# Issuing a kernel's loads from SyncE, ScalarE and GpSimd instead of from SyncE

## The chip, the core and the metric

One core of a Trainium2 chip runs the whole kernel. The time is the device time of one execution in microseconds (us). Each of the core's engines takes its instructions in order from a queue of its own: PE (TensorE), DVE (VectorE), ACT (ScalarE), POOL (GpSimd) and SP (SyncE, which only issues transfers here).

## The reference

Three layers follow each other. The first is gated linear attention over 4 batches, 8 heads, 768 tokens and a head dimension of 48:

```python
f = 1.0 / (1.0 + np.exp(-f_logit))
for t in range(S):
    state = f[:, :, t, :, None] * state + np.einsum('bhd,bhe->bhde', k[:, :, t], v[:, :, t])
    y[:, :, t] = np.einsum('bhd,bhde->bhe', q[:, :, t], state)
```

Its output, as a 3072 x 384 matrix x, goes through two MLP layers of width 2048:

```python
h = x @ w_in;  g = np.maximum(h, 0.0) + alpha * np.minimum(h, 0.0);  x = g @ w_out     # layer 0
h = x @ w_in;  g = h - np.tanh(h);                                   out = g @ w_out   # layer 1
```

The weights come as 64-bit floats; the activations and the output are 32-bit.

## The kernel before

The attention is cut into 24 steps. Step i handles 128 tokens (chunk c) of one batch b, with `c, b = divmod(i, 4)`, so steps 0 to 3 are the first chunk of the four batches. Their four outputs together are one tile of 512 tokens, on which layer 0 can start. MLP slots then run on PE (18 products of 128x512 each), and the later steps are spread among them.

A step has stages, and each engine does its part of them in order:

- `f` (`attn_f`): PE turns f (`ft`), ACT takes the exponential into the one buffer `gate` (L266) and adds 1 (L268), DVE scans it forward (`up`, L272) and backward (`down`, L280). The next step's L266 overwrites `gate`, so it waits for both scans.
- `k` (`attn_k`): PE turns k and q (`kt`, `qt`), DVE multiplies them into `kd` and `qd`.
- `s0`, `s1` (`attn_s`): PE forms the scores `sc` and turns `kd`. In steps 0 to 3 ACT copies the scores to `a` (L324) and POOL masks them (affine select, L325).
- `y0`, `y1` (`attn_y`): PE multiplies `a` with v; in steps 0 to 3 ACT and DVE write the result to x (L359, L360).
- `m` (`attn_m`): PE and DVE bring the state forward.

Weights come in 16 halves a layer (`load_w`, 768 KB each: the input half in four transfers for layer 0, the output half in one). `convert` turns such a half from 64-bit floats into two 32-bit parts: ACT takes the absolute value (`mag`, L54), DVE does five operations on it. Three raw buffers rotate, so the fourth half is loaded when the first has been converted.

A step's f, k, q and v are 192 KB each. In steps 0 to 3 f, k and q come as two transfers of 96 KB each, which a loop over `h` writes (heads `h::2`, four of the eight, with four tokens in a row, 768 bytes at a time):

```python
in_=a[b, h::2, t0:t0 + C, :].rearrange("p (t j) d -> p t (j d)", j=4)
```

From step 4 on each is one transfer of 192-byte rows (L175), into buffers that rotate over three steps: `f1`, `k1`, `q1` hold step 1, then step 4, then step 7. Steps 0 to 3 have their v loaded by `load_v` (one transfer of 144 KB in 192-byte rows and two of 24 KB in 64-byte rows).

Three things set the order. The table `PROLOGUE` says in which order the program's first parts are written: ("l", i) loads f, k and q of step i (from step 4 on v too), ("v", i) loads v, ("w", n) and ("c", n) load and convert half n of layer 0's weights, ("a", 0) loads alpha, and the rest are stages. A scheduler then places every engine's instructions by its own estimate of their times. And each transfer is given one of eight semaphores in turn; a transfer waits, in the queue of the engine that issues it, until the transfer that had its semaphore before has landed. SP and ACT share eight such semaphores (DMAHW0 to DMAHW7); POOL has eight of its own (DMASW0 to DMASW7).

Before the change SP issues every load and store but three: the second halves of step 0's f, k and q are issued by ACT.

Of the kernel before, what the change touches and what calls it, by code (L numbers as in the profile page):

```python
# [18 lines left out]
B, H, S, D = 4, 8, 768, 48  # L19
NT, DM, DFF = B * S, H * D, 2048  # L20
C = 128
# [11 lines left out]
HALF = 8  # L33

PROLOGUE = (
    ("l", 0), ("a", 0), ("l", 1), ("v", 0), ("l", 2), ("w", 0), ("v", 1), ("l", 3), ("v", 2), ("w", 1), ("w", 2),
    ("f", 0), ("k", 0), ("s0", 0), ("f", 1), ("s1", 0), ("y0", 0), ("y1", 0), ("m", 0), ("v", 3), ("k", 1), ("s0", 1),
    ("f", 2), ("s1", 1), ("y0", 1), ("y1", 1), ("m", 1), ("l", 4), ("k", 2), ("s0", 2), ("c", 0), ("f", 3), ("s1", 2),
    ("l", 5), ("y0", 2), ("y1", 2), ("m", 2), ("k", 3), ("s0", 3), ("l", 6), ("w", 3), ("s1", 3), ("y0", 3),
    ("y1", 3), ("c", 1), ("m", 3), ("f", 4),  # L40
)
GF = 256
# [28 lines left out]
def tile_main(tc, q, k, v, f_logit, w1_in, w1_out, alpha, w2_in, w2_out, out, flag):  # L71
    nc = tc.nc
    with ExitStack() as ctx:
# [23 lines left out]
            out=causal, in_=causal, compare_op=ALU.is_ge, fill=0.0,  # L97
# [13 lines left out]
        for b in range(2):  # L111
            t = const.tile([128, NP, 2, HW], F32, name=f"blocks{b}")
# [8 lines left out]
        alpha_raw = const.tile([FC, 128], F32, name="alpha_raw")  # L121


        def set_idle(t, nm):
            for a, b in ((4 * D, PAD), (PAD + 4 * D, H * HW)):
                nc.vector.memset(t[:, a:b], 30.0 if nm == "f" else 0.0)

        padded = {}
        for nm in ("f", "k", "q"):
            padded[nm] = []  # L130
            for j in range(NV):
                t = const.tile([128, H * HW], F32, name=f"{nm}{j}")
# [15 lines left out]
        def load_step(i):  # L148
            c, b = divmod(i, B)
            t0 = c * C  # L150
            s = {}
            for nm, a in (("f", f_logit), ("k", k), ("q", q), ("v", v)):
                if nm == "v" and c == 0:
                    continue
                if nm == "v":
                    t = s[nm] = ld.tile([128, H, D], F32, tag=nm, name=nm, bufs=NV)
                else:
                    if i == NV:
                        t = tp.tile([128, H * HW], F32, **{"f": dict(tag="g"), "k": dict(tag="g"), "q": dict(tag="neg", bufs=1)}[nm], name=nm)
                        set_idle(t, nm)  # L160
                    else:
                        t = padded[nm][i % NV]
                    if i < EARLY:

                        s[nm] = t[:, 0:2 * PAD].rearrange("p (h x) -> p h x", h=2)
                        for h in range(2):
                            (nc.scalar if i == 0 and h else nc.sync).dma_start(  # L167
                                out=s[nm][:, h, 0:4 * D],
                                in_=a[b, h::2, t0:t0 + C, :].rearrange("p (t j) d -> p t (j d)", j=4),
                            )  # L170
                        continue

                    s[nm] = t.rearrange("p (h x) -> p h x", h=H)
                    t = s[nm][:, :, 0:D]
                nc.sync.dma_start(out=t, in_=a[b, :, t0:t0 + C, :].rearrange("h t d -> t h d"))  # L175
            steps[i] = s

        def load_v(i):

            b = i  # L180
            s = steps[i]
            s["v"], s["v3"] = first_v[b % NV]
            nc.sync.dma_start(out=s["v"][:, :, 0:D], in_=v[b, 0:6, 0:C, :].rearrange("h t d -> t h d"))
            for h in range(2):
                nc.sync.dma_start(
                    out=s["v3"][:, h, :, D:64], in_=v[b, 6 + h, 0:C, :].rearrange("t (r d) -> t r d", r=3)
                )

# [2 lines left out]
        def load_w(m, g, half):  # L191
            wi, wo = ((w1_in, w1_out), (w2_in, w2_out))[m]
            f0 = g * GF
            a = stg.tile([128, 768, 2], I32, tag="raw", name="raw")
            raws[m, g, half] = a
            if half:
                nc.sync.dma_start(
                    out=a.rearrange("p (m e) w -> p m (e w)", m=2),
                    in_=wo[f0:f0 + GF].rearrange("(m p) e w -> p m (e w)", p=128),
                )  # L200
            elif m == 0:

                for h in range(2):
                    r0 = 64 * h
                    nc.sync.dma_start(
                        out=a[r0:r0 + D].rearrange("p (m f) w -> p m (f w)", m=3),
                        in_=wi[0:288, f0:f0 + GF].rearrange("(m p) f w -> p m (f w)", p=96)[D * h:D * h + D],
                    )
                    nc.sync.dma_start(
                        out=a[r0 + D:r0 + 64].rearrange("p (m f) w -> p m (f w)", m=3),  # L210
                        in_=wi[288 + D * h:288 + D * h + D, f0:f0 + GF].rearrange("(m p) f w -> p m (f w)", p=16),
                    )
            else:
                nc.sync.dma_start(
                    out=a.rearrange("p (m f) w -> p m (f w)", m=3),
                    in_=wi[:, f0:f0 + GF].rearrange("(m p) f w -> p m (f w)", p=128),
                )
# [340 lines left out]
        def stage(st, i, palloc=narrow):  # L558
            if st == "f":
                attn_f(i, palloc)  # L560
            elif st == "k":
                attn_k(i, palloc)
            elif st in ("s0", "s1"):
                attn_s(i, int(st[1]), palloc)
            elif st in ("y0", "y1"):
                attn_y(i, int(st[1]), palloc)
            else:
                attn_m(i, palloc)
# [4 lines left out]
        def convert(m, n):  # L573
            convert_a(m, *halves[n])
            convert_b(m, *halves[n])

        def load(m, n):
            load_w(m, *halves[n])

        for ev in PROLOGUE:  # L580
            if ev[0] == "c":
                convert(0, ev[1])
            elif ev[0] == "w":
                load(0, ev[1])
            elif ev[0] == "l":
                load_step(ev[1])
            elif ev[0] == "v":
                load_v(ev[1])
            elif ev[0] == "a":
                nc.sync.dma_start(out=alpha_raw, in_=alpha.rearrange("(c p) -> c p", p=128))  # L590
            else:
                stage(*ev, wide)

# [9 lines left out]
        for i in range(B, NC * B):  # L603
            c, b = divmod(i, B)

            if c < 3:
                t0, order = (0.7, 24.7)[c - 1] + 1.85 * b, tight_order
            else:
                t0, order = (c - 1) * FC + 3 * b + (2.5 if c == 3 else 0.5), wide_order
            for st, t in order:  # L610
                if ("f", i) not in PROLOGUE or st != "f":
                    put(t0 + t, stage, st, i)
            if i >= B + NV:
                put(t0 - NV * (1.85 if c < 3 else 3) + 0.8, load_step, i)
        first = sum(ev[0] == "c" for ev in PROLOGUE)
        when = {2: 0, 3: 1.2, 4: 2.0, 5: 3.2, 6: 4.2, 7: 5.4}
        for n in range(2 * NG):
            t = when.get(n, 7.5 + 1.5 * (n - NG)) if n >= first else -0.3
# [10 lines left out]
        for n, (g, half) in enumerate(halves):  # L629
            t = max(last + 6 + 1.5 * n, last + 2 * g + 2 * half + 2.2)  # L630
# [132 lines left out]
def kernel(tc, *args):  # L763
    nc = tc.nc
    with tc.tile_pool(name="flag", bufs=1) as fp:
        flag = fp.tile([1, 1], I32, name="flag")
        tile_main(tc, *args, flag)
        strong = nc.values_load(flag, min_val=0, max_val=1)
        with tc.If(strong > 0):
            tile_general(tc, *args)  # L770
# [33 lines left out]
```

## Time and profile before

| | us |
|---|---|
| median of 3 runs | 978.15 |
| lowest and highest | 977.35, 979.97 |
| the profiled execution, its whole time | 977.85 |
| its span, first to last instruction | 975.8 |

The span is what the trace covers; 2.05 us of the profiled execution lie outside it. In the trace an engine's line such as L359 is a line of the kernel, "SPq" and "ACTq" are the queues of SP and ACT while they issue a transfer, and PEclk is the granted share of TensorE's clock.

### The profile page before, as it was taken

How to read it: one execution, taken by the hardware profiler on the slowest of the kernel's cores; microseconds unless marked ns; L12 is line 12 of the kernel's file. 1: busy time of each engine (PE TensorE's matmuls, PEld its weight loads, DVE VectorE, ACT ScalarE, POOL GpSimd, SP SyncE). 2: the span in 40 equal slices, each digit the busy share in tenths (PEclk: the TensorE clock that was granted, in tenths of full speed). 3: DMA queues.
4: the chain of work that ended last, by engine and by line, in shares of the span. 5: the costliest groups of instructions: out<-in, count | busy, mean ns of one | idle time of the engine just before them, and what ended most of it. 6: DMA issues, size and time to landing. Idle time of an engine off the chain costs nothing.

```text
span 975.8 us, 13398 instructions
## 1 busy us (share of the span) xinstructions
PE 943.2 (97%) x5299; PEld 779.7 (80%) x5299; DVE 560.9 (57%) x926; ACT 408.4 (42%) x721; POOL 9.6 (1%) x24
## 2 busy tenths in 40 slices
PE   5598999999999999999999999999999999999997
PEld 5577787888888887888888888888888888888896
DVE  5589998566655565456444899953343433433432
ACT  3265556444444443444344665532232332322222
POOL 2000000000000000000000000000000000000000
PEclk9789999999999999999999999999999999999999
DMA  4897845042421232112022336330030110200201
GB/s 103 149 190 162 148 107 116 9 110 44 82 50 33 49 85 47 25 36 62 8 67 65 122 105 194 98 65 0 1 66 1 22 44 0 33 1 1 33 1 35
DMA packets 154277, 62.68 MB, mean 64 GB/s; under 512 B 123856, under 2 KB 141664, under 8 KB 154208
## 3 DMA queue, kind: packets, MB, share of 16 engines
q1 hardware_dynamic: 153812, 61.47, 28.4%
q8 instruction: 43, 0.70, 0.3%
q10 hardware_dynamic: 396, 0.29, 0.1%
q14 instruction: 26, 0.21, 0.1%
HBM read 49.55 MB, written 10.22 MB: 61 GB/s over the span
## 4 chain that ended last, share of the span: by engine, by line
PE 90%; DMA 4%; DVE 3%; SPq 2%; issue 0%; ACT 0%; ACTq 0%; DVEq 0%
PE acc L511 40%; PE h L451 13%; PE h L452 13%; PE h L453 13%; PE sc L319 2%; PE y L366 2%; PE y L342 2%; DMA k<-in_k_dram 2%; PE kt L248 1%; DMA raw<-in_moe_w_in_dram 1%; PE m L401 1%; PE qt L248 1%; PE ft L248 1%; SPq L167 1%; PE kr L305 1%; DMA f<-in_f_logit_dram 1%
## 5 line engine op out<-in xcount | busy, mean ns | idle before, releaser
L451 PE MATMUL h<-x,wih 128*128 128x512 f32 x576 | 228.6, 397 | 2.4 <-DMA x<-x 2.4
L452 PE MATMUL h<-x,wih 128*128 128x512 f32 x576 | 225.0, 391 | 0.0
L453 PE MATMUL h<-x,wil 128*128 128x512 f32 x576 | 225.0, 391 | 0.0
L511 PE MATMUL acc<-gh,wol 128*128 128x512 f32 x528 | 206.8, 393 | 1.8 <-DVE wol L233 1.8
L511 PE MATMUL acc<-gl,woh 128*128 128x512 f32 x528 | 207.6, 393 | 0.0
L511 PE MATMUL acc<-gh,woh 128*128 128x512 f32 x528 | 201.4, 396 | 0.9 <-ACT woh L232 0.9
L472 ACT CAST gh<-g 128x512 fp32r<-128x512 f32 x192 | 119.2, 621 | 139.4 <-DVE g L464 73.6
L473 DVE TENSOR_TENSOR gl<-g,gh 128x512 fp32r<-128x512 f32 x192 | 132.1, 688 | 76.5 <-ACT gh L472 67.9
L464 DVE TENSOR_TENSOR g<-h,g 128x512 f32<-128x512 f32 x96 | 66.2, 689 | 146.0 <-ACT g L463 146.0
L459 DVE SCALAR_TENSOR_TENSOR g<-neg,alpha_neg,g 128x512 f32<-128x512 f32 x96 | 72.0, 750 | 123.1 <-ACT neg L458 123.0
L463 ACT ACTIVATE g<-h 128x512 f32<-128x512 f32 x96 | 57.5, 599 | 174.8 <-PE h L453 174.8
L451 PEld LDWEIGHTS h<-x,wih 128*128 128x128 f32 x576 | 108.2, 188 | 24.6 <-DMA x<-x 2.8
L453 PEld LDWEIGHTS h<-x,wil 128*128 128x128 f32 x576 | 108.1, 188 | 23.2 <-DVE dec L65 0.2
L452 PEld LDWEIGHTS h<-x,wih 128*128 128x128 f32 x576 | 108.3, 188 | 20.9
L511 PEld LDWEIGHTS acc<-gh,wol 128*128 128x128 f32 x528 | 99.3, 188 | 22.6 <-DVE wol L233 1.9
L511 PEld LDWEIGHTS acc<-gh,woh 128*128 128x128 f32 x528 | 99.1, 189 | 22.9 <-ACT woh L232 1.5
L511 PEld LDWEIGHTS acc<-gl,woh 128*128 128x128 f32 x528 | 99.6, 189 | 20.4 <-DVE gl L473 0.4
L457 ACT ACTIVATE g<-h 128x512 f32<-128x512 f32 x96 | 57.5, 598 | 130.5 <-PE h L453 129.6
L458 ACT ACTIVATE neg<-h 128x512 f32<-128x512 f32 x96 | 56.9, 593 | 0.0
L272 DVE TENSOR_TENSOR_SCAN up<-gate,reset 128x516 f32<-128x516 f32 x24 | 29.5, 1231 | 10.5 <-ACT gate L268 9.9
L319 PEld LDWEIGHTS sc<-qd,kd 48*128 48x128 f32 x384 | 26.5, 193 | 9.0 <-issue 4.6
L319 PE MATMUL sc<-qd,kd 48*128 48x128 f32 x384 | 31.4, 291 | 1.2 <-DVE qd L294 1.2
(99 smaller groups left out, 805.8 us busy)
## 6 DMA issues: line engine op xcount, KB each, us to landing
raw<-in_moe_w_out_dram SPq DMA_DIRECT2D x16, 768.0 KB
raw<-in_moe_w_in_dram SPq DMA_DIRECT2D x8, 768.0 KB
raw<-in_moe_w_in_dram SPq DMA_DIRECT2D x16, 288.0 KB
x1d<-o SPq DMA_DIRECT2D x24, 192.0 KB
x1raw<-x1d SPq DMA_DIRECT2D x6, 768.0 KB
f<-in_f_logit_dram SPq DMA_DIRECT2D x20, 192.0 KB
k<-in_k_dram SPq DMA_DIRECT2D x20, 192.0 KB
q<-in_q_dram SPq DMA_DIRECT2D x20, 192.0 KB
```

The lines of the kernel that those rows point to most:

```text
L319: nc.tensor.matmul(out=sc[h][:, p], lhsT=s["kd"][r, p], rhs=s["qd"][r, p], start=True, stop=True)
L451: nc.tensor.matmul(out=h, lhsT=a, rhs=xh[:, r], start=(r == 0), stop=False)
L452: nc.tensor.matmul(out=h, lhsT=a, rhs=xl[:, r], start=False, stop=False)
L453: nc.tensor.matmul(out=h, lhsT=b, rhs=xh[:, r], start=False, stop=(r == 2))
L457: nc.scalar.activation(out=g, in_=h, func=ACTF.Relu)
L458: nc.scalar.activation(out=neg, in_=h, func=ACTF.Relu, scale=-1.0)
L459: nc.vector.scalar_tensor_tensor(out=g, in0=neg, scalar=alpha_neg[:, fc:fc + 1], in1=g, op0=ALU.mult, op1=ALU.add)
L463: nc.scalar.activation(out=g, in_=h, func=ACTF.Tanh)
L464: nc.vector.tensor_tensor(out=g, in0=h, in1=g, op=ALU.subtract)
L472: nc.scalar.copy(out=gh, in_=g)
L473: nc.vector.tensor_tensor(out=gl, in0=g, in1=gh.bitcast(F32), op=ALU.subtract)
L511: nc.tensor.matmul(out=t, lhsT=a, rhs=b, start=first and i == 0, stop=final and i == 2)
```

## The change

The loads are shared out among three engines. SP keeps the other loads of f, k and q, v from step 4 on, and all stores. ACT issues the second halves of f, k and q of steps 0 and 1 and the first input half of layer 0's weights. POOL issues v of steps 0 to 3, alpha and the other weights of layer 0. The weights of layer 1 stay on SP (`eng` is `nc.sync` where `m` is 1). `PROLOGUE` lists the first loads in another order and converts the first half two places later.

```diff
 PROLOGUE = (
-    ("l", 0), ("a", 0), ("l", 1), ("v", 0), ("l", 2), ("w", 0), ("v", 1), ("l", 3), ("v", 2), ("w", 1), ("w", 2),
+    ("l", 0), ("l", 1), ("w", 0), ("v", 0), ("v", 1), ("l", 2), ("v", 2), ("l", 3), ("w", 1), ("a", 0), ("w", 2),
     ("f", 0), ("k", 0), ("s0", 0), ("f", 1), ("s1", 0), ("y0", 0), ("y1", 0), ("m", 0), ("v", 3), ("k", 1), ("s0", 1),
-    ("f", 2), ("s1", 1), ("y0", 1), ("y1", 1), ("m", 1), ("l", 4), ("k", 2), ("s0", 2), ("c", 0), ("f", 3), ("s1", 2),
-    ("l", 5), ("y0", 2), ("y1", 2), ("m", 2), ("k", 3), ("s0", 3), ("l", 6), ("w", 3), ("s1", 3), ("y0", 3),
+    ("f", 2), ("s1", 1), ("y0", 1), ("y1", 1), ("m", 1), ("l", 4), ("k", 2), ("s0", 2), ("f", 3), ("s1", 2),
+    ("l", 5), ("c", 0), ("y0", 2), ("y1", 2), ("m", 2), ("k", 3), ("s0", 3), ("l", 6), ("w", 3), ("s1", 3), ("y0", 3),
...
-                            (nc.scalar if i == 0 and h else nc.sync).dma_start(
+                            (nc.scalar if i < 2 and h else nc.sync).dma_start(
...
-            nc.sync.dma_start(out=s["v"][:, :, 0:D], in_=v[b, 0:6, 0:C, :].rearrange("h t d -> t h d"))
+            nc.gpsimd.dma_start(out=s["v"][:, :, 0:D], in_=v[b, 0:6, 0:C, :].rearrange("h t d -> t h d"))
             for h in range(2):
-                nc.sync.dma_start(
+                nc.gpsimd.dma_start(
...
+            eng = nc.sync if m else nc.scalar if (g, half) == (0, 0) else nc.gpsimd
             if half:
-                nc.sync.dma_start(
+                eng.dma_start(
...
-                nc.sync.dma_start(out=alpha_raw, in_=alpha.rearrange("(c p) -> c p", p=128))
+                nc.gpsimd.dma_start(out=alpha_raw, in_=alpha.rearrange("(c p) -> c p", p=128))
```

The other transfers of `load_w` change in the same way to `eng.dma_start`. One line is added, so lines from L197 on are one higher in the changed kernel.

Three queues change at the places below. In a row, DMA is a transfer, out<-in are the program's tiles with their numbers, and [waits ...] names the semaphores that the instruction waits for.

On ACT, at the start of the program, before: three transfers, then the table load and the exponential of step 0 (`gate<-ft`).

```order
L167 DMA f0_129<-in_f_logit_dram 128x1x192
L167 DMA k0_138<-in_k_dram 128x1x192
L167 DMA q0_147<-in_q_dram 128x1x192
L266 ACT_TABLE_LOAD
L266 ACTIVATE gate_109<-ft_224 128x4x128 [waits PE_49]
```

The same place after the change: seven more transfers stand ahead of the table load. Six of them wait for an earlier transfer, and the last one's semaphore was that of `q1_150`, the second half of step 1's q.

```order
L167 DMA f1_132<-in_f_logit_dram 128x1x192
L167 DMA k1_141<-in_k_dram 128x1x192 [waits DMAHW1_49]
L167 DMA q1_150<-in_q_dram 128x1x192 [waits DMAHW3_49]
L206 DMA raw_181<-in_moe_w_in_dram 48x3x512 [waits DMAHW5_49]
L210 DMA raw_181<-in_moe_w_in_dram 16x3x512 [waits DMAHW7_49]
L206 DMA raw_181<-in_moe_w_in_dram 48x3x512 [waits DMAHW1_49]
L210 DMA raw_181<-in_moe_w_in_dram 16x3x512 [waits DMAHW3_49]
L267 ACT_TABLE_LOAD
L267 ACTIVATE gate_109<-ft_224 128x4x128 [waits PE_49]
```

So the first exponential has moved behind the landing of step 1's q. Further down on ACT, the exponentials of steps 1 and 2 now both stand ahead of the first copy of scores; before, only that of step 1 did.

On SP, from step 4's f on, before (`f1`, `k1`, `q1` and `v_425` are step 4, `f2` and so on step 5, `f0` and so on step 6):

```order
L175 DMA f1_132<-in_f_logit_dram 128x8x48
L175 DMA k1_141<-in_k_dram 128x8x48
L175 DMA q1_150<-in_q_dram 128x8x48
L175 DMA v_425<-in_v_dram 128x8x48
L175 DMA f2_135<-in_f_logit_dram 128x8x48
```

And after:

```order
L175 DMA f1_132<-in_f_logit_dram 128x8x48
L175 DMA v_425<-in_v_dram 128x8x48
L175 DMA v_493<-in_v_dram 128x8x48
L175 DMA f0_129<-in_f_logit_dram 128x8x48
L175 DMA f2_135<-in_f_logit_dram 128x8x48
L175 DMA k0_138<-in_k_dram 128x8x48
L175 DMA q0_147<-in_q_dram 128x8x48
L175 DMA v_571<-in_v_dram 128x8x48
L175 DMA k1_141<-in_k_dram 128x8x48
L175 DMA q1_150<-in_q_dram 128x8x48
```

Seven whole transfers, v of steps 4, 5 and 6, f of steps 6 and 5 and k and q of step 6, have moved between step 4's f and step 4's k. On PE the first product of step 4's `kt` stands ahead of step 3's scores, in both orders.

On POOL, after the memsets of the start, before: the masks of step 0 and of step 1, each two instructions.

```order
L142 MEMSET vb2_165 128x6x48
L325 AFFINE_SELECT a_265<-a_265 128x512 [waits Activation_49] x2
L325 AFFINE_SELECT a_356<-a_356 128x512 [waits Activation_49] x2
```

And after, from the end of the first weights on: ahead of these rows stand nine transfers of v, alpha and the four of the second input half, so 15 with the row of `raw_222`.

```order
L198 DMA raw_222<-in_moe_w_out_dram 128x2x768 [waits DMASW6_49]
L326 AFFINE_SELECT a_265<-a_265 128x512 [waits Activation_49] x2
L183 DMA va0_156<-in_v_dram 128x6x48 [waits DMASW7_49,PE_49]
L185 DMA vb0_157<-in_v_dram 128x3x16 [waits DMASW0_49,PE_49]
L185 DMA vb0_157<-in_v_dram 128x3x16 [waits DMASW1_49,PE_49]
L326 AFFINE_SELECT a_356<-a_356 128x512 [waits Activation_49] x2
```

Step 0's mask has moved behind 15 transfers, and step 1's behind three more (v of step 3, into the buffer that step 0 leaves).

## Rows read from the trace of the kernel before

**Rows 1.** The page's head: span and PE's busy time.

```profile
span 975.8 us, 13398 instructions
PE 943.2 (97%) x5299; PEld 779.7 (80%) x5299; DVE 560.9 (57%) x926; ACT 408.4 (42%) x721; POOL 9.6 (1%) x24
```

**Rows 2.** Windows by stage: length; busy time of PE, PEld, DVE, ACT, POOL; clock, DMA share, GB/s.

```profile
0.00:60.00 60.00, 38.81 (x469) 33.61 (x470) 32.43 (x82) 20.05 (x36) 9.64 (x24) 0.86 0.73 136
60.00:120.00 60.00, 54.95 (x396) 43.91 (x396) 57.33 (x99) 35.35 (x64) 0.00 (x0) 0.97 0.87 163
120.00:700.00 580.00, 580.00 (x3208) 474.06 (x3207) 368.13 (x594) 268.62 (x481) 0.00 (x0) 1.00 0.27 67
```

**Rows 3.** The chain that ended last, 41 to 51 us: start, us, what.

```profile
41.23 8.33 DMA k<-in_k_dram
49.70 0.73 PE kt L248 x4
```

**Rows 4.** Timeline of PE around steps 1, 3 and 4 and the first MLP product.

```profile
12.25 0.98 PE L253 MATMUL ft<-ident,f 128*64 128x128 f32 x13 [0.47 <-DMA f<-in_f_logit_dram]
50.35 2.08 PE L319 MATMUL sc<-qd,kd 48*128 48x128 f32 x16
59.04 0.48 PE L451 MATMUL h<-x,wih 128*128 128x512 f32 x1
```

**Rows 5.** Windows inside the loads of the start, columns as in rows 2.

```profile
6.00:8.00 2.00, 2.00 (x18) 1.74 (x16) 0.00 (x0) 0.20 (x1) 0.00 (x0) 1.00 0.27 92
10.00:12.00 2.00, 1.30 (x18) 0.85 (x16) 1.97 (x5) 0.00 (x0) 0.00 (x0) 1.00 0.28 91
36.00:50.00 14.00, 9.87 (x159) 8.92 (x156) 9.62 (x17) 6.34 (x12) 1.23 (x2) 0.98 1.06 189
42.00:44.00 2.00, 2.00 (x46) 2.00 (x46) 0.62 (x3) 1.83 (x3) 1.20 (x2) 1.00 0.98 334
50.00:56.00 6.00, 5.62 (x50) 4.73 (x50) 5.07 (x9) 2.56 (x5) 1.23 (x2) 0.51 1.24 180
58.00:60.00 2.00, 2.00 (x22) 1.74 (x19) 1.75 (x4) 1.36 (x3) 0.00 (x0) 1.00 1.47 179
```

**Rows 6.** Timeline of SP's queue where it issues step 6's loads.

```profile
51.94 1.13 SPq L175 DMA_DIRECT2D f<-in_f_logit_dram  x1
53.12 1.11 SPq L175 DMA_DIRECT2D k<-in_k_dram  x1
```

**Rows 7.** Timeline of ACT, 0 to 60 us.

```profile
3.25 1.28 ACT L266 ACT_TABLE_LOAD   x1 [3.25 <-issue]
7.80 0.60 ACT L266 ACTIVATE gate<-ft 128x512 f32<-128x512 f32 x1 [3.26 <-PE ft L253]
8.43 0.72 ACT L268 ACTIVATE gate<-gate,ones 128x512 f32<-128x512 f32 x1
15.07 1.06 ACT L324 COPY a<-sc 128x512 f32<-128x512 f32 x2
...
21.60 0.48 ACT L359 CAST x<-y 128x384 fp32r<-128x384 f32 x1 [2.06 <-PE y L358]
...
36.90 0.48 ACT L359 CAST x<-y 128x384 fp32r<-128x384 f32 x1 [11.14 <-PE y L358]
...
45.78 0.48 ACT L359 CAST x<-y 128x384 fp32r<-128x384 f32 x1 [1.57 <-PE y L358]
...
57.48 0.48 ACT L359 CAST x<-y 128x384 fp32r<-128x384 f32 x1 [3.89 <-PE y L358]
```

**Rows 8.** Timeline of DVE: first and last of eight instructions of one step.

```profile
37.41 0.56 DVE L360 TENSOR_TENSOR x<-y,x 128x384 fp32r<-128x384 f32 x1 [8.84 <-ACT x L359]
...
42.12 0.14 DVE L285 COPY inv<-carry 128x4 f32<-128x4 f32 x1
```

**Rows 9.** Timeline of POOL: its last memset and its first masks.

```profile
3.52 0.34 POOL L142 MEMSET vb<- 128x288 f32 x1
15.71 2.74 POOL L325 TENSOR_SCALAR_AFFINE_SELECT a<-a 128x512 f32<-128x512 f32 x2 [11.85 <-ACT a L324]
23.61 1.23 POOL L325 TENSOR_SCALAR_AFFINE_SELECT a<-a 128x512 f32<-128x512 f32 x2 [5.16 <-ACT a L324]
```

**Rows 10.** Timeline of DVE beside POOL's first masks.

```profile
17.95 0.53 DVE L285 COPY inv<-carry 128x4 f32<-128x4 f32 x1
```

**Rows 11.** Line L183's issues from SP: duration in ns, least, median, most.

```profile
L183 SPq DMA_DIRECT2D va<-in_v_dram x4: 401/720/1873, 11.3 to 38.2; - x4
```

## What the change is expected to do

> **What bounds the kernel now.** I read the page's head first. PE is busy 943.2 of 975.8 us [rows 1], so the question is where its 32.6 idle microseconds lie. The windows by stage answer it [rows 2]: 60 − 38.81 = 21.2 us idle in the first 60 us, 60 − 54.95 = 5.05 us in the next 60, and none from 120 to 700, where PE is busy 580 of 580 us. No transfer is late there, so nothing that the change does to loads can help there. In 60 to 120 us DVE works 57.33 of 60 us: what comes late into that stretch finds no slack to make it good. The start alone is at stake, and its end is the moment at which step 3's x lets the first MLP product begin: the x copy at 57.48 [rows 7], `h` at 59.04 [rows 4]. From there the program is one dense run, so I let a shift of step 3's x pass whole into the end time.
>
> What does that x wait for? The chain that ended last [rows 3] shows PE waiting for step 4's k, not for a thing of step 3: the transfer, issued at 41.23, takes 8.33 us, and `kt` starts at 49.70. The reader should see in the timeline that the 16 score products `sc` of step 3 begin at 50.35 [rows 4], right behind `kt`: PE works in order, and the order puts step 4's `kt` ahead of step 3's scores. So step 3's x hangs on the landing of step 4's k, 57.48 − 49.70 = 7.8 us behind it.
>
> And what keeps that k? The windows inside the loads [rows 5]. While only first-step halves are loaded, 91 to 92 GB/s move at a DMA share of 0.27 to 0.28: about a quarter of the 16 DMA engines' time, since a transfer's slowest dimension is four heads. A half of 96 KB then takes 98.3 KB / 92 GB/s = 1.07 us, and 24 of them 25.7 us, whoever issues them. Weights run at 334 GB/s with a share of 0.98. The whole transfers of 192-byte rows run at 179 to 180 GB/s with shares above 1: there the DMA engines are full, and SP issues one about every 1.18 us [rows 6], which is their pace (196.6 KB / 179 GB/s = 1.10 us).
>
> **The change part by part.**
>
> *SP's order, the term that decides.* Seven whole transfers are moved ahead of step 4's k. Each takes 1.10 us at 179 GB/s, or 1.18 us by the pitch of SP's issues: 7 × 1.14 = 8.0 us. PE still has step 4's `kt` ahead of step 3's `sc`. So `kt` goes from 49.70 to 57.7, and step 3's x from 57.48 to 65.5.
>
> *What could pay some of it back.* SP no longer issues v and weights, so it can reach step 4's f sooner than now. But the DMA engines have to move the same bytes first. The busiest quarter of them carries 25.7 us of halves and its share of the rest: 3.54 MB (three weight halves of 786 KB, four v of 197 KB, f and k of step 4), 18.7 us at the 189 GB/s of the mixed stretch from 36 to 50 us [rows 5]. The 8th half landed at 12.25 [rows 4], 3.7 later than 8 × 1.07, which is start and latency. 25.7 + 18.7 + 3.7 = 48.1, against a landing at 49.6 now: 1.5 us are idle there to be won. With the weights at 334 and the rest at 179 GB/s it is 7.1 + 6.6 instead of 18.7, and 6.5 us to be won; the mixed rate is the nearer row. A second refund: from 50 to 56 us the granted clock is 0.51, the lower level of 1.2 GHz, after PE had waited for transfers [rows 5]. If PE comes out of its wait at the full level, the 7.1 us from `sc` to x might lose 3 us. A surcharge: if the fourth weight half, on POOL, gets ahead of k, 786 KB / 334 GB/s = 2.4 us more. The bounds of this part are 8.0 − 6.5 − 3.0 = −1.5 and 8.0 + 2.4 = +10.4 us. I take +8.0: before, too, PE came out of its waits at the lower level, and the 1.5 and the 2.4 work against each other.
>
> The Trainium skill has a rule on this ("DMA: Bandwidth & Descriptors", "Issuing engines are not separate DMA queues"): transfers from any engine end up on the same 16 DMA engines, and several issuers save only the issuing time. The trace agrees as far as SP's issues go at the pace of the bytes; taken alone the rule gives a change of nothing, the third rival below.
>
> *ACT: ten transfers ahead of the first exponential.* The last of them waits for the landing of step 1's second q, the 12th half. The 8th (step 1's second f) had landed at 12.25 [rows 4], four more take 4 × 1.07 = 4.3: 16.5 us. One issue of 0.40 [rows 11] and the table load of 1.28 [rows 7] give step 0's `gate` at 18.2, not 7.80: 10.4 us later. Then the exponentials of steps 1 and 2 stand ahead of the first copy of scores, and each waits for both scans of the step before, which is a run of eight DVE instructions, 37.41 to 42.26 or 4.8 us [rows 8]. So step 2's `gate` is at 18.2 + 9.7 = 27.9, the copies to `a` come 1.32 (0.60 + 0.72) later at 29.2, and x of step 0, which lies 21.60 − 15.07 = 6.5 us behind them now [rows 7], comes between 32.4 (copies 1.06, masks 1.23, about 1 for the products) and 35.7. The next three x follow at a pitch between the DVE's 5.2 (4.8 and some 0.4 for the state) and the 8.9 us from 36.90 to 45.78 [rows 7]; the middle is 7. Step 3's x by this chain alone: 34.0 + 21 = 55.0, bounds 48.0 and 62.4. All are below 65.5, so the delayed exponential costs nothing as long as k binds; without that cover it would cost up to 62.4 − 57.5 = +4.9.
>
> *POOL: 15 transfers ahead of step 0's mask.* They hold 5264 separate runs (v: 3 × 768 and 6 × 384; alpha 16; weights 384 and 256). Nothing in before shows what POOL takes to issue. From below: SP's issues of one such v transfer take 0.40 to 1.87, median 0.72 us [rows 11], at least 0.5 ns a run. From above: POOL's own work per element, 0.34 us for 288 elements (1.2 ns) and up to 2.74 us for a pair of masks of 512 (2.7 ns) [rows 9]. With POOL free at 3.9, and 0.5 us a transfer: 3.9 + 7.5 + 5264 × 0.5 to 2.7 ns = 14 to 26 us. Step 0's `a` is not there before 29, so the issues are hidden; I take nothing. They show from the point at which the mask comes later than 65.5 − 21 − 5.9 (mask to x, 15.71 to 21.60) = 38.6 us, which is 5.2 ns a run.
>
> *v, alpha and the first conversion.* v now comes past SP's queue, and the first half is converted two places later. Both lie inside the steps' pitch, whose bounds of 5.2 and 8.9 us hold them; the wait for k covers both.
>
> The sum is 977.85 (the profiled execution's own time, 0.3 below the median of 978.15) + 8.0 = 985.9, or **986**.
>
> **The rivals.**
>
> *POOL issues slowly.* For it: DVE and POOL do disturb each other. A COPY of 128×4 elements on DVE took 0.53 us beside POOL's mask [rows 10], and 0.14 elsewhere [rows 8]; DVE is busy most of the time in which POOL would issue. Against it: nothing in before prices such an issue. At 8 ns a run the mask starts at 3.9 + 7.5 + 42.1 = 53.5, x of step 0 at 59.4, of step 3 at 80.4: +22.9, or about 1001. It decides from 5.2 ns a run. The Trainium skill speaks for this one ("SBUF — State Buffer", the "DVE blocks DMA" trap under "SBUF: two separate sides"): the runs of a GpSimd transfer are written by its own cores, which DVE can lock out. No transfer of before is issued by POOL, so no row shows it.
>
> *Faster.* The DMA share in the first 16 us is far below 1 (0.27 and 0.28 where I looked [rows 5]). If three queues fill that idle share with weights and v better than my 1.5 us, step 4's k lands by 49.8 in spite of its seven forerunners, and PE comes to `sc` at the full clock. Then ACT's chain decides: step 3's x at 55.0 down to 48.0, −2.5 to −9.5, about 973. It decides only when all 8 us are hidden. Against it: the busy quarter has no such idle time.
>
> *No change.* The seven transfers are hidden so, but ACT's late chain eats the gain: x of step 3 within 2.9 us of 57.48, some 977 to 979.
>
> **How the numbers follow.** Forecast 0.54, slow POOL 0.21, faster 0.12, no change 0.13. About 0.3% (2.9 us) is what a measurement of this kernel can tell from no change. The likeliest case's own range is 976.4 to 988.3 (−1.5 and +10.4). The range for 8 in 10 reaches down to 976, which leaves out the faster case, and up to 1002, where the slow POOL case stands at 8 ns a run; what is dearer, some 0.08, is left out. Faster 0.12, same 0.13, slower 0.75, since the forecast and the slow POOL are both slower.
>
> **What would show it.** Right: PE waits at step 4's `kt` for a transfer of k until about 57; step 0's `gate` stands at 18 to 21; the first `h` comes at about 67; 120 to 700 us is as full as now. Wrong: step 4's k lands by 50; or PE's long wait is for POOL's `a`, with POOL's issues longer than 2 us each; or the gap at ACT's first exponential is long past 21, so that the last wait is for a scan rather than for k. If the first `h` shifts and the end doesn't shift with it, the step "no slack in 60 to 120" is the one that failed.

## The result, and the profile after

The changed kernel took 988.22 us (median of 4 runs, 987.13 to 988.82), beside 979.06 for the kernel before in the runs taken with it: a ratio of 1.0092, 95% interval 1.0068 to 1.0115. It is slower, 2.2 us above the forecast of 986 and inside its range. The profiled execution took 988.82 us with a span of 987.0, so 11.2 us of span lie between the two traces. By the medians it is 9.2 us: single executions of the kernel before lie between 975.75 and 981.67 us, so 2 us between two spans are within their spread.

The page's head of the changed kernel, as [rows 1]:

```profile
span 987.0 us, 13426 instructions
PE 945.2 (96%) x5299; PEld 780.4 (79%) x5299; DVE 561.9 (57%) x926; ACT 409.6 (41%) x721; POOL 41.9 (4%) x73
```

PE does the same 5299 products. Its idle time grew from 32.6 to 41.8 us. The windows by stage, as [rows 2]:

```profile
0.00:60.00 60.00, 35.36 (x422) 29.14 (x422) 30.45 (x76) 18.31 (x32) 23.49 (x43) 0.86 0.66 148
60.00:120.00 60.00, 56.83 (x434) 45.95 (x434) 55.61 (x100) 33.78 (x61) 10.57 (x18) 0.97 0.75 139
120.00:700.00 580.00, 573.67 (x3173) 468.99 (x3171) 369.50 (x594) 270.27 (x484) 7.85 (x13) 1.00 0.28 69
```

The first 60 us hold 3.5 us less of PE's work, and behind 120 us, where PE had been full, 6.33 us are idle now. Where the start went is read from the timelines. ACT first (ACTq is its queue while it issues a transfer):

```profile
11.20 0.37 ACTq L206 DMA_DIRECT2D raw<-in_moe_w_in_dram  x1
13.41 0.32 ACTq L210 DMA_DIRECT2D raw<-in_moe_w_in_dram  x1
16.98 0.32 ACTq L206 DMA_DIRECT2D raw<-in_moe_w_in_dram  x1
20.01 0.32 ACTq L210 DMA_DIRECT2D raw<-in_moe_w_in_dram  x1
20.36 1.28 ACT L267 ACT_TABLE_LOAD   x1 [20.36 <-DMA raw<-in_moe_w_in_dram]
21.66 0.60 ACT L267 ACTIVATE gate<-ft 128x512 f32<-128x512 f32 x1
...
36.61 0.48 ACT L360 CAST x<-y 128x384 fp32r<-128x384 f32 x1 [2.75 <-PE y L359]
...
48.15 0.48 ACT L360 CAST x<-y 128x384 fp32r<-128x384 f32 x1
...
55.45 0.46 ACT L360 CAST x<-y 128x384 fp32r<-128x384 f32 x1
...
63.74 0.48 ACT L360 CAST x<-y 128x384 fp32r<-128x384 f32 x1 [5.55 <-PE y L359]
```

Against [rows 7] the first exponential has gone from 7.80 to 21.66 us, and step 0's x from 21.60 to 36.61. Each of the last four issues takes only 0.3 us, but stands 2.2 to 3.6 us behind the one before it: ACT is held by the semaphore of an earlier transfer. Step 3's x has gone from 57.48 to 63.74, only 6.3 us. The timeline of PE, as [rows 4]:

```profile
38.49 0.40 PE L254 MATMUL ft<-ident,f 128*64 128x128 f32 x2 [0.90 <-DMA f<-in_f_logit_dram]
39.74 0.98 PE L254 MATMUL ft<-ident,f 128*64 128x128 f32 x13 [0.84 <-DMA f<-in_f_logit_dram]
...
55.66 0.27 PE L249 MATMUL kt<-ident,k 128*128 128x128 f32 x1
55.86 1.16 PE L320 MATMUL sc<-qd,kd 48*128 48x128 f32 x16
...
65.20 0.48 PE L452 MATMUL h<-x,wih 128*128 128x512 f32 x1
...
106.36 1.16 PE L320 MATMUL sc<-qd,kd 48*128 48x128 f32 x16 [0.72 <-DVE qd L295]
...
123.55 1.16 PE L320 MATMUL sc<-qd,kd 48*128 48x128 f32 x16 [2.49 <-DVE qd L295]
...
129.39 0.76 PE L452 MATMUL h<-x,wih 128*128 128x512 f32 x1 [3.84 <-DMA x<-x]
```

The line at 55.66 is the one on which the forecast rested: step 4's `kt` starts with no wait ahead of it. Its k was there by then. PE's waits at 38.49 and 39.74 are for step 3's f, which had landed at 32.6 in the kernel before. The chain that ended last says the same: three f transfers, and then work. ACT's early transfers and its late first exponential are not on it.

```profile
2.93 9.64 DMA f<-in_f_logit_dram
12.59 14.31 DMA f<-in_f_logit_dram
...
27.56 12.14 DMA f<-in_f_logit_dram
...
39.74 0.92 PE ft L254 x13
```

The first `h` moved by 65.20 − 59.04 = 6.16 us, the end by 11.2. Of the 5.0 us in between, 4.0 are seen as waits of PE behind `h`: the rows of such waits up to 145 us add up to 9.0 us after the change (the last three above and 0.89, 0.90 and 0.20) and to 5.0 before. Before the change there are four of them, the last two being these:

```profile
87.06 1.17 PE L511 MATMUL acc<-gh,wol 128*128 128x512 f32 x3 [1.81 <-DVE wol L233]
119.68 0.47 PE L451 MATMUL h<-x,wih 128*128 128x512 f32 x1 [2.36 <-DMA x<-x]
```

POOL's issues, last, whose price nothing had shown:

```profile
17.88 0.82 POOL L183 DMA_DIRECT2D va<-in_v_dram  x1 [5.05 <-issue]
...
20.18 0.53 POOL L591 DMA_DIRECT2D alpha_raw<-in_moe_alpha_dram  x1
...
27.34 0.74 POOL L198 DMA_DIRECT2D raw<-in_moe_w_out_dram  x1
32.85 2.14 POOL L326 TENSOR_SCALAR_AFFINE_SELECT a<-a 128x512 f32<-128x512 f32 x2 [4.78 <-ACT a L325]
```

A transfer of 768 runs takes POOL 0.82 us, one of 16 runs 0.53: 0.3 us for 752 runs, or 0.4 ns a run. POOL was done at 28.1, with gaps of 4.3, 5.1 and 4.4 us between its issues, and then waited for ACT's `a`.

### The profile page after: what moved, and what is told of

Read it like the earlier page. It is cut to its first block, busy times and chain, and to the rows that moved or that the text cites. A ratio compares the mean times of both kernels' runs of the same rounds, so it can differ in the third digit from the quotient of the medians.

```text
span 987.0 us, 13426 instructions
## 1 busy us (share of the span) xinstructions
PE 945.2 (96%) x5299; PEld 780.4 (79%) x5299; DVE 561.9 (57%) x926; ACT 409.6 (41%) x721; POOL 41.9 (4%) x73
## 4 chain that ended last, share of the span: by engine, by line
PE 88%; DMA 5%; DVE 5%; ACT 1%; issue 1%; SPq 1%; DVEq 0%; ACTq 0%
PE acc L512 39%; PE h L452 13%; PE h L454 13%; PE h L453 13%; DMA f<-in_f_logit_dram 4%; PE sc L320 2%; PE y L367 2%; DMA x<-x 2%; PE y L343 1%; PE kt L249 1%; PE m L402 1%; PE qt L249 1%; PE ft L249 1%; DVE down L281 1%; PE kr L306 1%
```

## The experiments

Three theories went into the runs. **A**: ACT's late first exponential sets the start. **B**: a second queue (POOL's weights above all) takes the DMA engines from SP's f, k and q. **C**: the forecast's, step 4's k lands late behind seven transfers. All ratios are to the kernel before, on the same chip. "x0" and "x3" are the x casts of steps 0 and 3 on ACT, `h` the first MLP product; times are from each run's profile. The intervals are 0.1 to 0.35% wide to either side, so the ratios alone don't tell two parts of 0.2% apart.

| run | what it is | ratio, 95% interval | x0 | x3 | h | span |
|---|---|---|---|---|---|---|
| before | | 1 | 21.60 | 57.48 | 59.04 | 975.8 |
| after | | 1.0092, 1.0068 to 1.0115 | 36.61 | 63.74 | 65.20 | 987.0 |
| e1 | after, weights but the first on SP | 1.0065, 1.0039 to 1.0091 | 36.09 | 63.12 | 64.23 | 982.4 |
| e3 | after, ACT's part undone | 1.0097, 1.0066 to 1.0127 | 46.13 | 64.73 | 65.84 | 985.3 |
| e4 | after, table of before | 1.0054, 1.0037 to 1.0071 | 37.30 | 61.15 | 63.12 | 982.1 |
| e5 | before, table of after | 1.0040, 1.0024 to 1.0056 | 28.21 | 60.80 | 63.10 | 980.1 |
| f1 | before, v and alpha on POOL | 1.0017, 1.0003 to 1.0031 | 28.67 | 58.47 | 60.44 | 977.3 |
| f2 | before, weights but the first on POOL | 1.0027, 1.0014 to 1.0040 | 21.81 | 57.29 | 60.14 | 979.5 |
| f3 | before, ACT's part alone | 1.0015, 1.0003 to 1.0027 | 35.05 | 58.29 | 60.25 | 979.7 |
| f4 | before, first conversion later | 0.9972, 0.9953 to 0.9990 | 22.90 | 54.14 | 56.23 | 972.9 |
| f5 | before, first loads in the new order | 1.0013, 1.0001 to 1.0024 | 28.39 | 62.11 | 63.43 | 977.8 |
| g1 | after, first loads in the old order | 1.0114, 1.0081 to 1.0147 | 36.74 | 62.86 | 63.97 | 987.4 |
| g7 | after, step 4's k and q on ACT | 1.0166, 1.0139 to 1.0193 | 45.55 | 69.52 | 70.63 | 989.3 |
| g5 | e1, step 4's k and q on ACT | 1.0157, 1.0122 to 1.0192 | 47.04 | 71.17 | 72.28 | 990.1 |

### One part undone, or one half of the change alone (e1, e3, e4, e5)

**e1**, on the changed kernel:

```diff
-            eng = nc.sync if m else nc.scalar if (g, half) == (0, 0) else nc.gpsimd
+            eng = nc.scalar if (m, g, half) == (0, 0, 0) else nc.sync
```

> All weight halves but the first go back from GpSimd to SyncE, the rest stays as after the change. Theory A (ScalarE's late first exponential decides): the first exponential still stands at 20 to 22 us, the first MLP product at 64 to 66, about 986 to 989. Theory B (weights on a queue of their own take the DMA engines from f, k and q on SyncE's queue): step 3's f lands by 35 instead of 39.7, the x<-x transfers get short again, 979 to 982. Theory C (the prediction: step 4's k stands behind seven transfers): the seven are still there, 986 to 990.

It came out between: 984.47 us, with an interval that overlaps that of the changed kernel. Step 3's f was no longer waited for (`ft` at 37.01 without a wait), as B said. But then PE waited where C had put the wait, for step 4's k (timeline of PE):

```profile
56.30 0.30 PE L249 MATMUL kt<-ident,k 128*128 128x128 f32 x1 [3.79 <-DMA k<-in_k_dram]
```

So B's wait was real, and C's stands right behind it: taking one away laid the other bare, and step 3's x moved only from 63.74 to 63.12. Most of the 4.6 us between the two spans lies behind `h` (span less `h` is 918.2 instead of 921.8): the wait for x<-x at the second slot is 1.09 instead of 3.84 us.

**e3**, on the changed kernel:

```diff
-                            (nc.scalar if i < 2 and h else nc.sync).dma_start(
+                            (nc.scalar if i == 0 and h else nc.sync).dma_start(
...
-            eng = nc.sync if m else nc.scalar if (g, half) == (0, 0) else nc.gpsimd
+            eng = nc.sync if m or (g, half) == (0, 0) else nc.gpsimd
```

> Step 1's second halves and the first weight half go back from ScalarE to SyncE, v, alpha and the other weights stay on GpSimd. Theory A: the first exponential is back at about 8 us, the first MLP product at 58 to 60, 978 to 983. Theory B: step 3's f still lands near 39, 985 to 988. Theory C: k of step 4 stands ahead of most of the seven here, so 978 to 980.

987.77 us: nothing gained that could be measured, though the first exponential is back at 7.89 us (by f3, below, ACT's part is worth 0.15%, less than this interval can tell). A as the only cause has fallen, and so has C, which had asked for 978 to 980: step 4's k is issued right behind its f again, at 40.96 as against 41.23 before, and PE does not wait for it. B's forecast for this run fits. Timeline of PE and of SP's queue:

```profile
39.69 0.66 PE L254 MATMUL ft<-ident,f 128*64 128x128 f32 x2 [7.66 <-DMA f<-in_f_logit_dram]
```

```profile
21.56 5.85 SPq L167 DMA_DIRECT2D q<-in_q_dram  x2
27.45 6.27 SPq L167 DMA_DIRECT2D f<-in_f_logit_dram  x2
...
40.96 2.13 SPq L175 DMA_DIRECT2D k<-in_k_dram  x1
```

Two halves of 96 KB keep SP's queue for 5.85 and 6.27 us, just while POOL issues its weights (22.0 to 29.4 us in this run). With those weights on SP (e1) step 3's two f halves took this:

```profile
25.16 1.35 SPq L167 DMA_DIRECT2D f<-in_f_logit_dram  x2
```

The changed kernel differs from e1 in the weights' queue alone, and there they took this:

```profile
26.92 4.64 SPq L167 DMA_DIRECT2D f<-in_f_logit_dram  x2
```

PE, which works in order, has step 3's `ft` ahead of step 0's `y` here, so even step 0's x waited for that f (46.13). One more delay shows here. ACT's copies to `a` end at 17.8, but POOL masks step 0 only at 29.41, right behind its last issue; in the changed kernel ACT's lateness covers that.

```profile
28.66 0.74 POOL L198 DMA_DIRECT2D raw<-in_moe_w_out_dram  x1
29.41 1.24 POOL L326 TENSOR_SCALAR_AFFINE_SELECT a<-a 128x512 f32<-128x512 f32 x2
```

**e4** and **e5** split the change in two: e4 is the changed kernel with `PROLOGUE` as before, e5 the kernel before with `PROLOGUE` as after (the first hunk of the diff, taken out and put in alone).

> The issuers as after the change, the table PROLOGUE as before it. Theories A and B: the engines' share is untouched, 986 to 990. Theory C: SyncE still has seven transfers ahead of step 4's k, 985 to 990. If the table itself costs the time: 978 to 981.

> The table PROLOGUE as after the change, all issuers as before it. Theories A, B and C: first exponential at 8 us, one queue, step 4's k right behind its f, so 977 to 980. If the table itself costs the time: 984 to 988.

Neither half is free. The issuers alone cost 0.54%, the table alone 0.40%, together about the 0.92% of the change. All three theories had expected nothing of the table. In e5 PE's order has step 3's scores behind all of step 4's `kt` and `qt`; they start at 52.34 us, against 50.35 in [rows 4]. In e4 PE does wait for step 4's k:

```profile
55.09 0.63 PE L249 MATMUL kt<-ident,k 128*128 128x128 f32 x4 [1.00 <-DMA k<-in_k_dram]
```

### The parts one by one, on the kernel before (f1 to f5)

**f1** moves v and alpha, **f2** the weights but the first, **f3** is ACT's part. In f1 to f3 `PROLOGUE` is that of before.

```diff
f1, in load_v (three transfers) and for alpha
-            nc.sync.dma_start(out=s["v"][:, :, 0:D], in_=v[b, 0:6, 0:C, :].rearrange("h t d -> t h d"))
+            nc.gpsimd.dma_start(out=s["v"][:, :, 0:D], in_=v[b, 0:6, 0:C, :].rearrange("h t d -> t h d"))
f2, in load_w (each transfer with eng.dma_start)
+            eng = nc.sync if m or (g, half) == (0, 0) else nc.gpsimd
f3, in load_step and load_w
-                            (nc.scalar if i == 0 and h else nc.sync).dma_start(
+                            (nc.scalar if i < 2 and h else nc.sync).dma_start(
+            eng = nc.scalar if (m, g, half) == (0, 0, 0) else nc.sync
```

> Before the change, with v of the first steps and alpha alone issued by GpSimd. Theory A (ScalarE's late first exponential): nothing late, 976 to 979. Theory B (a second queue takes the DMA engines from f, k and q): v is small, so step 3's f at most 2 us late, 977 to 981. Theory C (step 4's k behind others on SyncE): its k stands right behind its f, 975 to 978.

> Before the change, with all weight halves of layer 0 but the first issued by GpSimd. Theory A: 976 to 979. Theory B: the weights run beside step 3's f, k, q and hold them up, step 3's f lands at 36 or later instead of 32.6, 981 to 986. Theory C: nothing ahead of step 4's k, and the weights no longer ahead of it on SyncE, 974 to 978.

> Before the change, with only ScalarE's part of it: second halves of step 1 and the first weight half. Theory A: the first exponential at 20 to 22 us, the first MLP product at 63 to 65, 982 to 986. Theory B: one more queue only for the first weight half, 977 to 980. Theory C: one v and two f stand between, step 4's k right behind its f, 977 to 980.

Each costs a little, 0.17%, 0.27% and 0.15%, and the three add up to 0.59%, near e4's 0.54%. With e5's 0.40% for the table the parts add up in the other runs too: 0.72% for e1 (0.65 measured), 0.84% for e3 (0.97) and 0.99% for the whole change (0.92), all inside the intervals. B's size for f2 was right at its lower end (981.80 us), but the transfer held up was another: step 1's v on SP, for which PE waited 12.42 us. Its timeline of POOL, of SP's queue and of PE:

```profile
20.72 0.74 POOL L198 DMA_DIRECT2D raw<-in_moe_w_out_dram  x1
```

```profile
24.23 8.37 SPq L185 DMA_DIRECT2D vb<-in_v_dram  x2
```

```profile
36.45 0.45 PE L355 MATMUL y<-a,va 128*64 128x128 f32 x1 [12.42 <-DMA va<-in_v_dram]
```

The same two `vb` transfers keep SP's queue for 1.5 to 3.0 us in the kernel before; here, with POOL's 1.5 MB of weights under way, for 8.37. f3 says how little A counts alone: step 0's x is 13.5 us late (35.05), and step 3's only 0.8 (58.29). A had asked for 982 to 986 and got 980.78.

**f4** moves only the first conversion to its new place in the table of before; **f5** has the new order of the first loads and the conversion at its old place.

```diff
f4
-    ("f", 2), ("s1", 1), ("y0", 1), ("y1", 1), ("m", 1), ("l", 4), ("k", 2), ("s0", 2), ("c", 0), ("f", 3), ("s1", 2),
-    ("l", 5), ("y0", 2), ("y1", 2), ("m", 2), ("k", 3), ("s0", 3), ("l", 6), ("w", 3), ("s1", 3), ("y0", 3),
+    ("f", 2), ("s1", 1), ("y0", 1), ("y1", 1), ("m", 1), ("l", 4), ("k", 2), ("s0", 2), ("f", 3), ("s1", 2),
+    ("l", 5), ("c", 0), ("y0", 2), ("y1", 2), ("m", 2), ("k", 3), ("s0", 3), ("l", 6), ("w", 3), ("s1", 3), ("y0", 3),
f5
-    ("l", 0), ("a", 0), ("l", 1), ("v", 0), ("l", 2), ("w", 0), ("v", 1), ("l", 3), ("v", 2), ("w", 1), ("w", 2),
+    ("l", 0), ("l", 1), ("w", 0), ("v", 0), ("v", 1), ("l", 2), ("v", 2), ("l", 3), ("w", 1), ("a", 0), ("w", 2),
```

> Before the change, with only the first conversion two places later in the table, which in TensorE's order puts step 3's scores ahead of step 4's kt. If the wait for step 4's k is what sets the start in the kernel before, its scores no longer stand behind it and 973 to 976 result. If the later conversion's work on VectorE stands in the way of step 3, 979 to 982.

> Before the change, with only the first loads in the new order (the first conversion at its old place). If the edits add up, the difference of e5 and f4, plus 6 to 7 us: 984 to 986. If the load order costs only together with the later conversion: 977 to 980.

f4 is faster than both kernels, 975.59 us. Its timeline of PE shows why:

```profile
48.42 1.16 PE L319 MATMUL sc<-qd,kd 48*128 48x128 f32 x16
49.52 0.66 PE L248 MATMUL kt<-ident,k 128*128 128x128 f32 x4
```

Step 3's scores now stand ahead of step 4's `kt`, do not wait for its k, and run at the full clock (1.16 us instead of 2.08 in [rows 4]). `h` comes 2.8 us sooner. So in the kernel before step 4's `kt`, standing ahead of the scores, did hold step 3 up, as the prediction had read it. Of this only a small part is a wait for k. PE's longer wait there is for step 4's f, as the kernel before shows:

```profile
48.01 0.52 PE L248 MATMUL ft<-ident,f 128*128 128x128 f32 x3 [2.27 <-DMA f<-in_f_logit_dram]
...
49.70 0.72 PE L248 MATMUL kt<-ident,k 128*128 128x128 f32 x4 [0.62 <-DMA k<-in_k_dram]
```

f5 cost 0.13%; the table's two edits together cost 0.40%, so f4's gain is lost beside f5, where the scores stand behind `qt` again.

### The first loads again, and step 4's k out of the queue (g1, g7, g5)

**g1** is the changed kernel with f4's table. **g7** is the changed kernel, and **g5** is e1, with this edit:

```diff
-                nc.sync.dma_start(out=t, in_=a[b, :, t0:t0 + C, :].rearrange("h t d -> t h d"))
+                (nc.scalar if i == 4 and nm in "kq" else nc.sync).dma_start(out=t, in_=a[b, :, t0:t0 + C, :].rearrange("h t d -> t h d"))
```

> After the change, with the first loads in the old order and the first conversion at its new, later place. If the edits add up: 988 minus 6 to 7, so 980 to 983. If the load order has no part in it once the engines share the transfers: 986 to 989.

> After the change, but k and q of step 4 are issued by ScalarE right behind step 0's scores, so that the seven transfers on SyncE's queue no longer stand ahead of them; TensorE's order stays. Theory C (the prediction's term of 8 us): the first MLP product comes 5 to 8 us earlier, 980 to 983. Theories A and B (the late start of the steps sets the end, and step 4's k is there in time as the trace of after shows): 986 to 989.

> As e1 (all weight halves but the first back on SyncE), with k and q of step 4 issued by ScalarE. Theory C: the wait of 3.8 us for step 4's k, which e1 showed, goes, 980 to 982. Theories A and B: the steps are late anyway, 984 to 986.

g1, 989.56 us: the sum over the edits failed. The order of the first loads makes no difference that can be measured in the changed kernel, and the later conversion, which gains 0.28% in f4, costs here: g1 and e4 differ in nothing else, 1.0114 against 1.0054, and their intervals do not touch. PE's order shows one reason. In e4 (shown first) step 3's `y` stands ahead of step 4's scores; in g1 eight of these scores stand ahead of it, and ahead of them a wait for step 4's q:

```profile
59.68 0.67 PE L355 MATMUL y<-a,va 128*64 128x128 f32 x8
...
61.04 0.93 PE L320 MATMUL sc<-qd,kd 48*128 48x128 f32 x10
```

```profile
57.63 0.63 PE L249 MATMUL qt<-ident,q 128*128 128x128 f32 x4 [1.51 <-DMA q<-in_q_dram]
...
59.04 1.11 PE L320 MATMUL sc<-qd,kd 48*128 48x128 f32 x8
60.08 1.33 PE L355 MATMUL y<-a,va 128*64 128x128 f32 x9
```

From step 3's exponential on ACT to its x it is 22.7 us in g1 and in the changed kernel, 20.3 in e4 and 20.2 before. Another reason lies further on. In g1, e1, e3 and the changed kernel, which all have the later conversion and shared issuers, PE waits about 2.5 us at 122 to 124 us for a later step's `qd` (in g7 and g5 at 129 to 130 us); e4 and f4 have no such wait.

g7 and g5 did not test C; they missed by more than any theory allowed. The transfer that was to be early waited for the semaphore of an earlier one, in ACT's own queue (timeline of ACT in g7):

```profile
33.25 0.71 ACT L314 COPY blocks<-state 48x192 f32<-48x192 f32 x2
45.10 0.40 ACTq L175 DMA_DIRECT2D k<-in_k_dram  x1
45.55 0.48 ACT L360 CAST x<-y 128x384 fp32r<-128x384 f32 x1 [11.59 <-DMA f<-in_f_logit_dram]
```

ACT stood for 11 us, and step 0's x behind it. From there the steps run with no wait for k: step 3's x follows 24.0 us (g7) and 24.1 us (g5) later. It is 23.2 in f3 and 27.1 in the changed kernel. Of these 3 to 4 us, PE's two waits for step 3's f (0.90 and 0.84) are 1.7; the rest was not taken apart.

## Why the prediction came out right, and where it did not

**The bound.** Right in part: the larger share of the loss arises in the start, and in the kernel before step 3's scores stand behind step 4's `kt` (f4). k itself was the smaller wait there, 0.62 us against 2.27 for step 4's f. That a shift passes just as it is was wrong (below), and 120 to 700 us, which was to stay as full as before, now holds 6.33 us of waits.

**Step 4's k, +8.0 us.** The size was near (+6.3 at step 3's x), the cause was not the one named: PE does not wait at that `kt`, which the prediction had given as its first sign of being right. By 55.66 us k had landed, so it came at most 6.1 us later than the 49.56 before, and PE reached its `kt` no sooner by itself. The step that failed is "`kt` goes from 49.70 to 57.7", and with it "the delayed exponential costs nothing as long as k binds". The mechanism is real: with the seven transfers ahead of it, k is waited for in e1 (3.79 us, `kt` at 56.30) and in e4 (1.00 us, `kt` at 55.09). But there `kt` comes 5.4 to 6.6 us later than at 49.70, not 8.0, and in the changed kernel other delays keep PE from it until k is there. So the total came out near by luck: 8.0 us for a wait that is not there, against 6.2 us at `h` from other causes and the loss behind `h`, which the sum put at nothing.

**ACT's chain.** Forecast for `gate` 18.2, measured 21.66: each of ACT's last transfers waits for a landing, and these came at a pitch of 2.2 to 3.6 us, not 1.07, with SP's and POOL's transfers under way beside them. x of step 0 at 36.61 (forecast 32.4 to 35.7), and from there 27.1 us to step 3's x instead of 21: the pitch of 7 was undersized, it is 7.7 to 8.0 in f3, g7 and g5, which wait for no f there, and the first pitch is 11.5 (9.8 to 10.5 in those three), with the wait for step 3's f in it. So this chain, that f and PE's new order, not k, set x of step 3. Step 3's exponential stands at 41.01 (37.27 before), 3.7 us late, and its x comes another 2.5 us later behind it. In e1, where the f is in time, the exponential stands at 39.15, and in e3, where ACT's chain starts early and the f is late, at 42.81: at most 1.9 us of the 3.7 are ACT's chain, and the late f is enough for all of it.

**POOL.** Right in the changed kernel: the issues are hidden, though only behind ACT's delay (e3). The price of 0.4 ns a run is just under the lower bound of 0.5, far from the 5.2 at which it would decide. The sum left out the gaps between the issues, which put their end at 28.1, past the 14 to 26 expected. The Trainium skill's trap of DVE locking out POOL ("SBUF — State Buffer", "SBUF: two separate sides") did not show in the issues of the start: the one at 10.57 in f1 took 0.85 us while DVE made step 0's `kd` (10.59 to 11.28), the one at 17.88 after the change 0.82 with DVE idle. Further on an effect of its kind shows, a small one. An issue of L210 that takes 0.52 us elsewhere took this in the changed kernel, beside a DVE operation of L57 (timelines of POOL and DVE):

```profile
159.88 0.90 POOL L210 DMA_DIRECT2D raw<-in_moe_w_in_dram  x1
```

```profile
160.11 0.56 DVE L57 TENSOR_SCALAR mag<-mag 128x768 f32<-128x768 f32 x1
```

In every run, each issue behind 70 us that is more than 0.06 us longer than others of its line has such a TENSOR_SCALAR of 128x768 beside it (others beside one are not longer). The surplus is at most 0.4 us, and no run shows that it costs time.

**The refunds and the rule.** Step 3's scores did run at the full clock (1.16 us at 55.86), but the refund didn't reach x, which came 8.1 us behind `kt` instead of 7.8: step 4's first scores (60.31) stand ahead of step 3's `y` in the new order of PE, and from 61 to 64 us, where that `y` runs, the granted clock is 0.51, the lower level of 1.2 GHz again, after PE had waited 1.16 us at 59.10 and 0.33 at 60.31. The Trainium skill's rule that all issuers end on the same 16 DMA engines ("DMA: Bandwidth & Descriptors", "Issuing engines are not separate DMA queues") was used for "no change". The runs differ from it in one point, that sharing by queue only saves issuing time: beside POOL's weights SP's queue was held (8.37 us in f2, 5.85 and 6.27 in e3), and f, k, q or v, which PE needed first, came late.

**A shift passes whole.** Too little: between the two traces `h` moved 6.16 us, the end 11.2. Of the other 5.0, 4.0 are seen as longer waits of PE, and most of the rest as PE's idle time behind 960 us (7.6 us against 6.4). 2.5 us are the wait for `qd` that goes with the later conversion beside shared issuers. The wait for x<-x, 3.84 (2.36 before), came while POOL issued a weight half (118.4 to 120.6 us), but e3 has weights on POOL too and waits 0.23 there, so that part stays open. f5 shows that a shift need not pass either: its `h` comes 4.4 us later than before, its end only 2.0.

What is not settled: why SP's queue is held so long beside POOL's weights (the runs show when and how long, not what the DMA engines choose by), why the two edits of the table cost more together (0.40%) than f4 and f5 apart, and what C alone would cost in the changed kernel, since g7 brought a wait of its own.

## What to carry to other kernels

Putting a transfer on another engine's queue takes away the one order that said what is needed first: big transfers that nobody waits for then run beside small ones that are waited for. And a transfer's wait for its semaphore stands in the queue of the engine that issues it, so an engine that computes should issue only what never has to wait. When undoing one part changes nothing, look in that run's trace for the next wait before calling the part innocent, and ask whether the runs could have told its price: delays lay side by side at step 3 here, and each group of transfers moved alone cost under 0.3%.

## What the runs showed of the hardware beyond what was expected

SP's issue of the same two small transfers took 1.5 to 3.0 us in the kernel before and 8.37 us with POOL's weights in flight (f2), step 3's two f halves 1.35 us (e1) and 6.27 us (e3). POOL's issue costs 0.53 us for 16 runs, 0.74 for a weight half of 256 and 0.82 for 768. The seven transfers added on ACT moved its first exponential by 13.9 us, of which their issuing itself is 3.4 us (the sum of the seven issues).
